# Converting float64 weights on chip: the scaled high words move from SBUF to a PSUM bank

## The chip, the cores and the metric

The kernel runs on one core of one Trainium2 chip. The metric is the device time of one execution in microseconds. One execution was also taken by the hardware profiler, and all rows below come from it. TensorE runs the matmuls and transposes; VectorE, ScalarE and GpSimd work element by element; SyncE (SP) issues nearly all DMAs. In profile rows the engines are PE (PEld for its weight loads), DVE, ACT, POOL and SP. SBUF is the working memory. PSUM has eight banks of 128 partitions by 512 float32; TensorE writes its results there, and VectorE and ScalarE reach it too.

## The reference

A top-k attention feeds two MLPs, one after the other:

```
scores = q k^T / sqrt(64)                    # 4 batches, 8 heads, 576 tokens
keep the 32 largest of each row, softmax over them, times v
x  = attention out as 2304 tokens by 512
x  = relu(x @ w_in)^2 @ w_out                # 512 -> 2048 -> 512
y  = h @ w_out, h = max(0.01 g, g), g = x @ w_in    # second pair of weights
```

q, k and v are float32. The four weight matrices arrive as float64, because the setup scales them by a float64 number, so the kernel has to make float32 of them on chip.

## The kernel before

Every operand of a matmul is split in two: a high part, rounded to TensorE's fp32r format, and the rest. Products are the sum of high by high, high by low and low by high.

**Attention.** 144 tiles of 128 query rows are worked in 72 pairs. A pair has 16 slots. In them VectorE finds the 32 largest of 576 scores of each row by four MAX8 (L800) with three MATCH_REPLACE8 (L802) between them. Around this, at fixed slots, come the scores (L278 on TensorE, evicted at L279), the threshold and exponential (L297, L298, L302), the normalisation (L311), the transposes (`pt_main`, four at L316 into one bank, read at L321 and L322; `pt_left`, L329, read at L338 and L339) and the product with v (`av_split`, L388, read at L393 and L394). In the first three units the older form without a split is used (L324, L342, `av` at L377).

**MLPs.** The tokens are six blocks. A block starts as soon as the attention has filled it, and its matmuls run between the attention's slots: for each of 16 chunks `f` of 128 hidden units, 12 matmuls at L552, then the activation (L562 to L573), then the second product (L590 or L592). A generator `moe` hands this out in small portions; `rate` says how many portions go into a slot.

**Weights.** The first block's 32 chunk steps (16 for each MLP) meet their weights as float64. `w_raw` (L462) loads two tiles of 128x512 double words a step into `wraw`, a ring of four. `w_convert_steps` makes float32 of each: ScalarE scales the low words into an integer (L486) and the high words as a float (L487), VectorE joins them in two bit passes (L490, L491), ScalarE rounds the result to its high part (L495) and GpSimd takes the difference (L498). `w_store` (L506, L507) writes the split chunk to DRAM, and later blocks only load it again (L514, L515). A step converts the chunk of two steps ahead. 64 tiles are converted in all, with 128 bit passes.

**Rings and order.** The two words of a conversion live in tiles of the tag `wc`, a ring of `WCB` slots, which the output tiles `y` (L606) share. Attention results in PSUM come from `bank()`, a ring of three banks under the tag `att`:

```
def bank():
    return psum.tile([P, 512], F, tag="att", name="att", bufs=3)
```

Transposes, value products and the scores of the batches that go straight on (other than batch 0) all take theirs there; the other five banks hold `h` and four `acc` from the first block on. Each engine works its instructions in the order that a planner wrote at build time, from priorities and modelled times; at run time only semaphores hold an instruction. `behind("dve")` puts the first bit pass behind the top-k instruction that was current when the code reached it, and `CONVP` gives conversions a lead in priority.

Of the kernel before, what the change touches and what calls it, by code (L numbers as in the profile page):

```python
# [8 lines left out]
F = mybir.dt.float32  # L9
R = mybir.dt.float32r  # L10
U = mybir.dt.uint32
AF = mybir.ActivationFunctionType
OP = mybir.AluOpType
# [6 lines left out]
H_SCALE = 2.0 ** -112  # L20
# [28 lines left out]
NS = 6  # L49
NE = 4  # L50
WRB = 4
WCB = 5
KRB = 1
VTB = 2

# [15 lines left out]
def topk_attention_moe_moe2_kernel(  # L71
# [12 lines left out]
    P = 128  # L84
# [8 lines left out]
    PE, ACT, DVE, POOL, SP = nc.tensor, nc.scalar, nc.vector, nc.gpsimd, nc.sync  # L93

    const = ctx.enter_context(tc.tile_pool(name="const", bufs=1))
    pool = ctx.enter_context(tc.tile_pool(name="work", bufs=2))
# [3 lines left out]
    def bank():  # L100
        return psum.tile([P, 512], F, tag="att", name="att", bufs=3)
# [7 lines left out]
    def behind(key):  # L109

        return tc.issue_after(cur[key].ins) if key in cur else ExitStack()
# [15 lines left out]
    for u in units:  # L127
        for hp in range(NHP):
# [4 lines left out]
            for t in range(2 * n // P):  # L133
                lo, hi = t * P, t * P + P
# [312 lines left out]
    def w_alloc(i):  # L447
        wi = pool.tile([P, 2, 512], R, tag="wi", name="wi", bufs=3)
        wo = pool.tile([P, 2, 512], R, tag="wo", name="wo", bufs=4)
        wt[i] = (wi, wo)  # L450
        return wi, wo
# [16 lines left out]
    def w_convert(i):  # L468
        g = w_convert_steps(i)
        while True:  # L470
            with tc.high_priority(offset=CONVP):
                if next(g, 1):
                    return
            yield

    def w_convert_steps(i):
        if i >= len(steps) or not fresh[i]:
            return
        w2 = w_alloc(i)
        for raw, w in zip(wraw.pop(i), w2):  # L480
            if W64:
                lo, hi = raw[:, :, 0], raw[:, :, 1]
                c = pool.tile([P, 512], F, tag="wc", name="wc", bufs=WCB)
                cu = c.bitcast(U)
                b = pool.tile([P, 512], U, tag="wc", name="wb", bufs=WCB)
                ACT.activation(b, lo, AF.Copy, scale=L_SCALE, bias=L_BIAS)  # L486
                ACT.activation(c, hi.bitcast(F), AF.Copy, scale=H_SCALE)  # L487
                yield 0
                with behind("dve"):
                    DVE.scalar_tensor_tensor(b, cu, 3, b, op0=OP.logical_shift_left, op1=OP.bitwise_or)  # L490
                DVE.scalar_tensor_tensor(cu, cu, 0x80000000, b, op0=OP.bitwise_and, op1=OP.bitwise_or)  # L491
                yield 0
            else:
                c = raw
            ACT.activation(w[:, 0, :], c, AF.Copy)  # L495
            yield 0
            with behind("pool"):
                POOL.tensor_tensor(w[:, 1, :], c, w.bitcast(F)[:, 0, :], op=OP.subtract)  # L498
            yield 0
# [30 lines left out]
    def moe(j, layer):  # L530
# [69 lines left out]
        for c in range(na):  # L600
# [4 lines left out]
            else:  # L605
                y = pool.tile([P, 512], F, tag="wc", name="y", bufs=WCB)  # L606
                ACT.activation(y, acc[c], AF.Copy)
# [18 lines left out]
    for uh in uhs:  # L626
        b, hp, i = uh["b"], uh["hp"], uh.get("di")
# [248 lines left out]
```

## Time and profile before

| | |
|---|---|
| time, median of 3 runs | 1259.81 us (1259.77 to 1260.94) |
| the profiled execution's own time | 1260.58 us |
| its span | 1258.8 us |
| TensorE busy | 1153.8 us, 92% |
| VectorE busy | 1001.0 us, 80% |
| ScalarE busy | 930.4 us, 74% |
| GpSimd busy | 761.4 us, 60% |
| mean granted TensorE clock | 0.96 |

A line of the kernel in a row (L490) is the line of the code above. `wb<-wc,wb` names the tile that is written and those that are read. Rows by line and shape give the count, the busy time in us and the mean ns of one instruction, then the engine's idle time just before them and what ended it. Rows of a timeline give start and duration in us. In rows of waits stand the total in us, how often, and the longest.

### The profile page before, as it was taken

Reading aid. Unit: us, or ns where it says so; the run is one execution under the profiler, and the core shown is the slowest. Engines: PE = TensorE matmul, PEld = TensorE weight load, DVE = VectorE, ACT = ScalarE, POOL = GpSimd, SP = SyncE. Lnnn points to the kernel's source line nnn. Section 1 sums busy time; section 2 is a strip of 40 time slices with the busy share of each in tenths; the row PEclk is TensorE's granted clock in tenths of the full one; section 3 lists DMA queues with packets and bytes.
Section 4 is the critical chain, followed back from the end, with each engine's and each line's share of the span. In section 5 each row is a group of like instructions: output and inputs, shape, how many; then the busy total and the mean of one; then the engine's idle time right before and its main releaser. Section 6 shows DMA issues by size and latency. Waiting matters only on the chain.

```text
span 1258.8 us, 20236 instructions
## 1 busy us (share of the span) xinstructions
PE 1153.8 (92%) x6352; PEld 1003.9 (80%) x6352; DVE 1001.0 (80%) x1944; ACT 930.4 (74%) x2031; POOL 761.4 (60%) x856
## 2 busy tenths in 40 slices
PE   4888877999868988998999999999999999999998
PEld 3666755787646776997899989888878889999897
DVE  7999999899999999899999999999999810111022
ACT  6999989899888896887788787877777754433322
POOL 7977697488778998447765576654466732003300
PEclk9889885999989998998999999999999999999999
DMA  9745468578776675898998878876666569878974
GB/s 309 259 166 202 155 230 275 191 268 287 254 253 220 234 241 179 286 341 262 374 367 289 298 260 285 281 237 230 214 206 217 190 235 362 285 251 318 358 258 142
DMA packets 110522, 323.24 MB, mean 257 GB/s; under 512 B 17488, under 2 KB 25680, under 8 KB 110416
## 3 DMA queue, kind: packets, MB, share of 16 engines
q1 hardware_dynamic: 107776, 317.24, 73.2%
q10 hardware_dynamic: 2640, 4.72, 1.0%
q8 instruction: 51, 0.84, 0.3%
q14 instruction: 55, 0.45, 0.1%
HBM read 254.54 MB, written 67.37 MB: 256 GB/s over the span
## 4 chain that ended last, share of the span: by engine, by line
PE 53%; DVE 28%; ACT 4%; issue 2%; DMA 2%; POOL 2%; ACTq 0%; POOLq 0%; DVEq 0%
PE h L552 22%; PE acc L592 12%; PE acc L590 9%; DVE m L800 8%; DVE w L802 7%; DVE wb L490 5%; DVE wc L491 4%; PE att L388 3%; PE att L316 3%; PE att L377 2%; DVE PTs L322 2%; PE sp L278 1%; PE att L329 1%; DMA sd<-stage 1%; DMA wo<-wd 1%
## 5 line engine op out<-in xcount | busy, mean ns | idle before, releaser
L552 PE MATMUL h<-xh,wi 128*128 128x512 f32 (+2 forms) x1280 | 349.4, 346 | 5.3 <-ACT ga L562 3.3
L800 DVE MAX8 m<-w 128x8 f32<-128x576 f32 x432 | 314.8, 748 | 1.8
L552 PEld LDWEIGHTS h<-xh,wi 128*128 128x128 f32 x1280 | 228.5, 192 | 33.3 <-ACT ga L562 3.7
L573 POOL TENSOR_TENSOR gl<-ga,gh 128x512 fp32r<-128x512 f32 (+2 forms) x160 | 168.8, 1055 | 125.7 <-ACT gh L572 67.3
L298 POOL TENSOR_TENSOR e<-s,e 128x576 f32<-128x576 f32 x144 | 210.2, 1480 | 39.9 <-ACT e L297 38.5
L802 DVE MATCH_REPLACE8 w<-m,w 128x576 f32<-128x576 f32 x288 | 213.0, 742 | 0.6
L552 PE MATMUL h<-xl,wi 128*128 128x512 f32 (+2 forms) x640 | 207.7, 343 | 2.1 <-DVE xl L604 1.9
L590 PE MATMUL acc<-gh,wo 128*128 128x512 f32 (+2 forms) x768 | 156.2, 344 | 2.3 <-ACT gh L572 2.1
L571 POOL TENSOR_TENSOR ga<-ga,gb 128x512 f32<-128x512 f32 (+2 forms) x80 | 84.4, 1055 | 116.4 <-ACT gb L570 116.0
L592 PE MATMUL acc<-wo,gh 128*128 128x512 f32 x576 | 152.0, 398 | 2.8 <-ACT gh L572 2.6
L590 PEld LDWEIGHTS acc<-gh,wo 128*128 128x128 f32 x768 | 126.6, 190 | 13.5 <-ACT gh L572 3.4
L552 PEld LDWEIGHTS h<-xl,wi 128*128 128x128 f32 x640 | 121.9, 192 | 15.1 <-DVE xl L604 4.2
L572 ACT ACTIVATE gh<-ga 128x512 fp32r<-128x512 f32 (+2 forms) x192 | 100.3, 522 | 35.7 <-POOL ga L571 24.1
L297 ACT ACTIVATE e<-s,kf 128x576 f32<-128x576 f32 x144 | 107.1, 780 | 20.1 <-POOL kf L290 14.4
L592 PEld LDWEIGHTS acc<-wo,gh 128*128 128x128 f32 x576 | 103.7, 188 | 22.6 <-ACT gh L572 4.8
L302 ACT ACTIVATE e<-e,kf 128x576 f32<-128x576 f32 x144 | 112.2, 780 | 11.6 <-POOL e L298 8.3
L311 ACT ACTIVATE e<-e,rc 128x576 f32<-128x576 f32 x144 | 104.4, 776 | 14.9 <-DVE rc L307 14.8
L562 ACT ACTIVATE ga<-h 128x512 f32<-128x512 f32 (+2 forms) x96 | 46.8, 487 | 85.3 <-PE h L552 81.5
L800 DVE MAX8 m<-s 128x8 f32<-128x576 f32 x144 | 105.2, 747 | 5.8 <-ACT s L279 5.6
L802 DVE MATCH_REPLACE8 w<-m,s 128x576 f32<-128x576 f32 x144 | 106.9, 743 | 0.6
L316 PE MATMUL att<-ident,e 128*128 128x128 f32 x576 | 92.0, 291 | 10.3 <-DVE xf L394 5.8
L278 PE MATMUL sp<-KTa,q 128*128 128x288 f32 x320 | 72.0, 355 | 28.7 <-ACT stage L279 22.3
(89 smaller groups left out, 2225.1 us busy)
## 6 DMA issues: line engine op xcount, KB each, us to landing
wi<-wd SPq DMA_DIRECT2D x160, 512.0 KB, 5.2
wo<-wd SPq DMA_DIRECT2D x160, 512.0 KB, 5.4
wraw<-in_w_dram SPq DMA_DIRECT2D x64, 512.0 KB, 4.8
sd<-stage SPq DMA_DIRECT2D x72, 288.0 KB, 3.1
s<-sd SPq DMA_DIRECT2D x72, 288.0 KB, 5.0
wd<-wi SPq DMA_DIRECT2D x32, 512.0 KB, 3.8
wd<-wo SPq DMA_DIRECT2D x32, 512.0 KB, 3.6
kraw<-in_k_dram SPq DMA_DIRECT2D x16, 576.0 KB, 4.6
```

The source lines that it names most:

```text
L297: ACT.activation(e, x, AF.Relu, bias=pr["kf"][:, i:i + 1], scale=-FAR)
L298: cur["pool"] = POOL.tensor_tensor(e, x, e, op=OP.subtract)
L302: ACT.activation(e, e, AF.Exp, bias=pr["nb"][:, i:i + 1], scale=0.125, accum_out=pr["sum"][:, i:i + 1])
L311: ACT.activation(e, e, AF.Copy, scale=pr["rc"][:, i:i + 1])
L316: PE.transpose(ps[:, j * P:(j + 1) * P], t["e"][:, j * P:(j + 1) * P], ident)
L552: PE.matmul(h[:, 0:n], lhsT=wi[:, w, c * P:(c + 1) * P], rhs=x[c][y][:, 0:n], start=cnt == 0, stop=cnt == 3 * NK - 1)
L572: ACT.activation(gh[:, 0:n], a[:, 0:n], AF.Copy)
L573: (DVE if j >= GLD else POOL).tensor_tensor(gl[:, 0:n], a[:, 0:n], gh.bitcast(F)[:, 0:n], op=OP.subtract)
L590: PE.matmul(acc[c][:, 0:n], lhsT=wo[:, w, cs], rhs=g[:, 0:n], start=first, stop=last)
L592: PE.matmul(acc[c], lhsT=g[:, cs], rhs=wo[:, w, :], start=first, stop=last)
L800: cur["dve"] = DVE.max(out=m8[:, x, 8 * r:8 * r + 8], in_=t["s"] if r == 0 else t["w"])
L802: cur["dve"] = DVE.match_replace(out=t["w"], in_to_replace=m8[:, x, 8 * r:8 * r + 8], in_values=t["s"] if r == 0 else t["w"], imm_value=NEG)
```

## The change

The scaled high words no longer go to an SBUF tile but to a bank of the attention's three. The low words keep a tile of the ring `wc`, in which both bit passes now write; each pass reads one PSUM and one SBUF operand where it read two SBUF operands. A conversion takes one slot of `wc` where it took two, and the ring has four slots in place of five. `c`, which L495 and L498 read, is now that SBUF tile seen as float32.

```
-WCB = 5
+WCB = 4
...
-                c = pool.tile([P, 512], F, tag="wc", name="wc", bufs=WCB)
-                cu = c.bitcast(U)
-                b = pool.tile([P, 512], U, tag="wc", name="wb", bufs=WCB)
+                b = pool.tile([P, 512], U, tag="wc", name="wc", bufs=WCB)
+                v = bank()
                 ACT.activation(b, lo, AF.Copy, scale=L_SCALE, bias=L_BIAS)
-                ACT.activation(c, hi.bitcast(F), AF.Copy, scale=H_SCALE)
+                ACT.activation(v, hi.bitcast(F), AF.Copy, scale=H_SCALE)
                 yield 0
+                vu, c = v.bitcast(U), b.bitcast(F)
                 with behind("dve"):
-                    DVE.scalar_tensor_tensor(b, cu, 3, b, op0=OP.logical_shift_left, op1=OP.bitwise_or)
-                DVE.scalar_tensor_tensor(cu, cu, 0x80000000, b, op0=OP.bitwise_and, op1=OP.bitwise_or)
+                    DVE.scalar_tensor_tensor(b, vu, 3, b, op0=OP.logical_shift_left, op1=OP.bitwise_or)
+                DVE.scalar_tensor_tensor(b, vu, 0x80000000, b, op0=OP.bitwise_and, op1=OP.bitwise_or)
                 yield 0
```

## Rows read from the trace of the kernel before

**Rows 1.** By stretch: busy us of PE, PEld, DVE, ACT, POOL; clock, DMA share, GB/s.

```profile
164.00:495.00 331.00, 277.90 (x1304) 220.53 (x1304) 319.48 (x517) 289.94 (x607) 273.84 (x232) 0.92 0.71 243
495.00:1000.00 505.00, 496.94 (x2883) 444.30 (x2882) 490.75 (x1030) 394.07 (x832) 306.72 (x369) 0.99 0.79 273
```

**Rows 2.** Chain that ended last, by line: 164 to 495, then 495 to 1259.

```profile
by line: DVE m L800 19.7%; DVE wb L490 18.3%; DVE w L802 17.8%; DVE wc L491 17.0%; issue 4.8%; DVE PTs L322 3.2%; PE att L377 3.1%; PE h L552 2.0%; DMA sd<-stage 1.8%; DVE PTs L339 1.1%; PE att L278 1.0%; DVE xf L394 0.9%; ACT wi L495 0.9%;
...
by line: PE h L552 35.6%; PE acc L592 19.8%; PE acc L590 14.9%; PE att L388 4.5%; DVE m L800 4.5%; DVE w L802 4.2%; PE att L316 3.4%; issue 1.6%; DVE PTs L322 1.2%; DMA wo<-wd 1.2%; POOL e L298 1.1%; PE att L329 1.0%; DMA wi<-wd 0.9%; PE at
```

**Rows 3.** TensorE's waits from 164 to 495 us.

```profile
PE att L278 <- DVE PTs L322: 13.1, 7, 5.5
```

**Rows 4.** VectorE's groups by line and shape, whole span.

```profile
L490 DVE SCALAR_TENSOR_TENSOR wb<-wc,wb 128x512 uint32<-128x512 uint32 x64 | 72.5, 1133 | 6.4 <-ACT wc L487 6.3
L322 DVE TENSOR_TENSOR PTs<-att,PTs 128x512 fp32r<-128x512 f32 x108 | 72.4, 678 | 3.4 <-ACT PTs L321 2.5
L491 DVE SCALAR_TENSOR_TENSOR wc<-wc,wb 128x512 uint32<-128x512 uint32 x64 | 70.2, 1098 | 0.5
...
L573 DVE TENSOR_TENSOR gl<-ga,gh 128x384 fp32r<-128x384 f32 x32 | 17.9, 559 | 62.6 <-ACT gh L572 60.7 <-issue 1.8
...
L604 DVE TENSOR_TENSOR xl<-acc,xh 128x384 fp32r<-128x384 f32 x4 | 2.1, 547 | 0.0
```

**Rows 5.** Lines L490 and L487: ns min/median/max, first and last start.

```profile
L490 DVE SCALAR_TENSOR_TENSOR wb<-wc,wb x64: 661/1118/1925, 164.2 to 489.4; 128x512 uint32<-128x512 uint32 x64
...
L487 ACT ACTIVATE wc<-wraw x64: 646/673/727, 25.7 to 484.9; 128x512 f32<-128x512 f32 x64
```

**Rows 6.** Timeline, two bit passes and a GpSimd instruction.

```profile
316.94 0.67 DVE L490 SCALAR_TENSOR_TENSOR wb<-wc,wb 128x512 uint32<-128x512 uint32 x1
317.01 1.74 POOL L573 TENSOR_TENSOR gl<-ga,gh 128x512 fp32r<-128x512 f32 x1
...
317.71 1.59 DVE L491 SCALAR_TENSOR_TENSOR wc<-wc,wb 128x512 uint32<-128x512 uint32 x1
```

**Rows 7.** Users of the tag att, 164 to 495 us, counts behind x.

```profile
L316 PE MATMUL att<-ident,e x128: 270/273/476, 176.4 to 486.2; 128*128 128x128 f32 x128
...
L279 ACT ACTIVATE s<-att x56: 388/411/503, 199.7 to 494.4; 128x288 f32<-128x288 f32 x56
...
L329 PE MATMUL att<-ident,e x30: 270/272/423, 177.9 to 470.0; 128*64 128x128 f32 x30
...
L393 ACT ACTIVATE tmp<-att x9: 376/381/438, 280.2 to 481.5; 64x256 f32<-64x256 f32 x8, 64x320 f32<-64x320 f32 x1
```

**Rows 8.** Timeline, first and last users of some banks, and one conversion.

```profile
176.37 1.76 PE L316 MATMUL att<-ident,e 128*128 128x128 f32 x7 [0.48 <-ACT e L311]
...
179.85 0.63 ACT L324 ACTIVATE PT<-att 128x512 f32<-128x512 f32 x1
...
304.86 0.60 PE L316 MATMUL att<-ident,e 128*128 128x128 f32 x4
...
308.89 1.07 ACT L321 ACTIVATE PTs<-att 128x512 fp32r<-128x512 f32 x2
...
311.23 0.71 ACT L487 ACTIVATE wc<-wraw 128x512 f32<-128x512 f32 x1
...
314.33 0.69 DVE L322 TENSOR_TENSOR PTs<-att,PTs 128x512 fp32r<-128x512 f32 x1
...
315.08 0.53 PE L278 MATMUL att<-KT,q 128*128 128x288 f32 x2 [0.24 <-DVE PTs L322]
...
316.34 0.39 ACT L279 ACTIVATE s<-att 128x288 f32<-128x288 f32 x1
...
316.59 1.11 PE L388 MATMUL att<-PTs,VT 128*128 128x256 f32 x8
...
333.18 0.41 DVE L394 TENSOR_TENSOR xf<-att,tmp 64x256 f32<-64x256 f32 x1
```

**Rows 9.** Users of the tag att, 0 to 164 us.

```profile
L324 ACT ACTIVATE PT<-att x26: 592/631/664, 34.6 to 162.5; 128x512 f32<-128x512 f32 x26
```

## Prediction, written before the change was run

> **What bounds the kernel now.** I first read the table of busy times by stretch, to find the stretch in which the change acts. All 128 bit passes lie between 164 and 492 us, so I cut the span at 164 and 495. In these 331 us VectorE is busy for 319.5, ScalarE for 289.9, TensorE for 277.9 (at a granted clock of 0.92) and GpSimd for 273.8; from 495 to 1000 TensorE is busy for 496.9 of 505 us [rows 1]. So VectorE leads up to 495 and TensorE afterwards. The chain of work that ended last, read by stretch, says the same. Up to 495 us its two largest owners besides the top-k lines L800 and L802 are the bit passes, L490 with 18.3% and L491 with 17.0%; behind 495 the MLP matmuls L552, L590 and L592 hold 70% [rows 2]. Together the passes are 35% of the chain in the stretch, some 117 of 331 us, and what is saved there should move everything behind it forward, because TensorE then has a fixed queue of matmuls and no gap to lose the gift in. Last I read the waits in the stretch: the longest of TensorE's are 13.1 us in which score matmuls wait for a bank that VectorE's L322 has not released [rows 3]. So the other engines' gaps, too, are VectorE being late.
>
> **The two passes.** They take 72.5 and 70.2 us, 1133 and 1098 ns each [rows 4], together 142.7 us. The mean hides two speeds: L490's shortest is 661 ns and its longest 1925 [rows 5]. The timeline shows when which comes: the pass at 316.94 us began just ahead of GpSimd's L573 (317.01) and took 0.67; the next, at 317.71, began while that L573 was running (until 318.75) and took 1.59 [rows 6]. It would have ended at 318.4 undisturbed and ended at 319.30, 0.6 behind the GpSimd instruction. So a pass over two SBUF tiles that starts under a running GpSimd instruction is held up until that is through. After the change each pass reads one tile from PSUM and one from SBUF. The nearest row of that kind and size is L322, 128x512 from a bank and an SBUF tile: 108 of them, mean 678 ns, in stretches where GpSimd is busy for 274 of 331 and 307 of 505 us [rows 1, 4]. I take 678 for both passes: 128 x 0.678 = 86.8 us, so VectorE gives back 142.7 - 86.8 = 55.9 us. Bounds: at the shortest pass, 661 ns, it is 58.1; if the stretching stayed as it is, nothing. I take the first end, since 108 rows of the same operands show no slow kind. A loss from the operand itself I exclude, by the next comparison.
>
> Does reading PSUM cost VectorE more? At 128x384, L573 reads two SBUF tiles and takes 559 ns (VectorE runs that line in the last block alone, by the constant GLD, behind the attention); L604 reads a bank and an SBUF tile and takes 547 [rows 4]. So the move costs the operation nothing. [...]
>
> **ScalarE.** L487 writes the bank instead of an SBUF tile. No row shows ScalarE writing PSUM; the nearest is L487 itself, 646 to 727 ns, median 673 [rows 5]. I keep 673; the ends are worth -1.7 and +3.5 us over 64. L495 and L498 read the result in SBUF as before, so they keep their price. The smaller ring (four slots in place of five) now serves one tile a conversion where it served two, four conversions in place of two and a half: no wait comes from it, and part of the waits for L491 at L486 and L487 should go. The DMAs of a step are the same; the loads at L462 reuse a raw tile when L487 has read it, so if L487 waits for a bank, SP's queue waits too, with the stores L506 and L507 and all else behind it.
>
> **GpSimd** gets back what the passes took from it; it is not a bound, so I count nothing.
>
> **What is late next.** Were VectorE alone the bound, the stretch would fall to 331 - 55.9 = 275 us. But ScalarE has 289.9 us of work in it and TensorE 277.9, so the gain is cut at 331 - 290 = 41. VectorE reached 96.5% of the stretch; ScalarE is fed by all the others, and I allow it 95%: 289.9 / 0.95 = 305, a gain of 26 us. Ends: 41 (no idle) and 0.
>
> **The banks.** This is the new cost: a wait for one of three banks, at L487 on ScalarE and in front of every attention matmul on TensorE, in whose queue the MLP's matmuls stand behind. The rows bound it. In the stretch there are 32 groups of four transposes, 15 pairs at L329, 56 score halves and 9 value products [rows 7]; the unsplit products at L377 I leave out. How long does each keep its bank? A transpose group from 176.37 to 180.48 us: 4.1; another from 304.86 until L322 ended at 315.02: 10.2. A score half from 315.08 to 316.73: 1.65. A value product from 316.59 to 333.59: 17 [rows 8]. A conversion would have kept one from L487 at 311.23 [rows 8] until the second pass ended at 319.30 [rows 6]: 8.1, or 7.2 with passes 0.44 us shorter each. Three banks offer 3 x 331 = 993 us. With the long holds, and pairs like transposes, the sum is 47 x 10.2 + 56 x 1.65 + 9 x 17 + 64 x 7.2 = 1186, that is 395 us of stretch: 64 us slower. With the short ones (4.1, 1.65, 4.1 for a value product, and 4.1 for a conversion, an estimate) it is 193 + 92 + 37 + 262 = 584, or 195 us, hidden. The middle is 885, 295 us, just at ScalarE's floor. I take the middle or better, since the long holds are mostly waits for VectorE (L322 ran 5.4 us behind the eviction of the same group), and VectorE is what gets faster; and since a conversion that waits has cover: the code converts two steps ahead of the matmuls, and 64 conversions in 331 us make a step of two 10.3 us, so some 20 us.
>
> **Sum.** The profiled execution took 1260.6 us (span 1258.8), 0.8 over the median of 1259.8. 1260.6 - 26 = 1234.6; I say 1234.
>
> **Rivals.** (a) *Banks decide, slower.* 176 groups share 993 bank-us, 5.6 us each; above that mean hold the stretch grows. At 6.2 us it is 364 us, 33 more than now, and the time 1294. For it: the 10.2 and 17 above, and TensorE's present waits for banks [rows 3]. Against: those holds come out of VectorE's lateness. [...] (b) *Early holds.* The first two conversions' high words are written from 25.7 us on, the first pass comes at 164.2 [rows 5]. If banks are taken as early, two of three are gone for 138 us; the 26 transpose groups of that time [rows 9] at 4.1, 13 pairs as long and some 20 us of products, 180 in all, would have to pass through one, so some 42 lost and 26 won: about 1277. Against: a bank comes from a ring that the attention uses all the time, not from a free buffer. (c) *VectorE's whole gain:* ScalarE's floor does not hold, because part of its 290 us (the score evictions that only fill a store for later) moves behind 495, where it is busy for 394 of 505 us [rows 1]: down to 1260.6 - 55.9 = 1205, so 1205 to 1221. (d) *The banks take most of it:* 1247 to 1262.
>
> **Chances.** Forecast, 1222 to 1246: 0.52. (c) 0.08. (d) 0.17, of which 0.08 is faster by over 0.2% and 0.09 within 0.2% (2.5 us, about what a measurement of this kernel can tell from no change). (a) 0.17 and (b) 0.06, both slower. So faster 0.68, same 0.09, slower 0.23. The range reaches from (c) to the near part of (a): 1211 to 1270, which leaves out about 0.06 below and 0.13 above. The forecast's own range is 1222 to 1246.
>
> **What would show it.** Right: both passes near 678 ns with no slow kind; the conversion ends near 469 instead of 495; VectorE's share in it falls below 90% while ScalarE's rises to about 95%; behind it TensorE stays full and the two kernels run parallel. Wrong: passes above 900 ns would break the first term; ScalarE idle at L487, released by L491 or L322, or TensorE idle in front of L278, L316 and L388 for more than some 50 us, means that the banks decide; L487 of the first conversions far ahead of their passes means (b).

## The result, and the profile after

The changed kernel takes 1221.9 us (median of 4 runs, 1220.9 to 1225.3) against 1259.8 for the kernel before: a ratio of 0.971 (95% interval 0.968 to 0.973), 38 us faster. The forecast was 1234, its own range 1222 to 1246, the whole range 1211 to 1270; the median lies at the lower edge of the forecast's own range. The profiled execution took 1220.9 us, its span is 1219.1.

VectorE's groups by line and shape come first, in the columns of [rows 4]:

```profile
L322 DVE TENSOR_TENSOR PTs<-att,PTs 128x512 fp32r<-128x512 f32 x108 | 72.7, 678 | 5.4 <-ACT PTs L321 4.6
L490 DVE SCALAR_TENSOR_TENSOR wc<-att,wc 128x512 uint32<-128x512 uint32 x64 | 43.4, 682 | 23.4 <-ACT att L486 22.7 <-POOL ga L571 0.3
L491 DVE SCALAR_TENSOR_TENSOR wc<-att,wc 128x512 uint32<-128x512 uint32 x64 | 43.2, 680 | 0.5
```

The passes fell from 1133 and 1098 ns to 682 and 680, 142.7 us to 86.6. The slow kind is gone altogether, as the rows by line show (ns min/median/max; L486 is now the line that writes the high words, L487 before):

```profile
L490 DVE SCALAR_TENSOR_TENSOR wc<-att,wc x64: 657/681/692, 184.8 to 437.3; 128x512 uint32<-128x512 uint32 x64
...
L491 DVE SCALAR_TENSOR_TENSOR wc<-att,wc x64: 660/679/692, 186.9 to 438.0; 128x512 uint32<-128x512 uint32 x64
...
L486 ACT ACTIVATE att<-wraw x64: 603/646/704, 183.2 to 436.6; 128x512 f32<-128x512 f32 x64
```

The last pass starts at 438.0 us. In the kernel before, the same line ran

```profile
L491 DVE SCALAR_TENSOR_TENSOR wc<-wc,wb x64: 666/1067/1912, 168.5 to 491.8; 128x512 uint32<-128x512 uint32 x64
```

so the conversions are done 54 us sooner. The first two high words no longer run 138 us ahead of their passes: L486 starts at 183.2, L490 at 184.8.

Busy time by stretch, in the columns of [rows 1]; 456 lies as far from the end as 495 did before:

```profile
164.00:456.00 292.00, 267.01 (x1298) 217.05 (x1296) 240.67 (x461) 274.14 (x577) 224.81 (x226) 0.96 0.83 285
456.00:961.00 505.00, 492.70 (x2870) 439.92 (x2871) 498.92 (x1052) 397.40 (x846) 306.89 (x365) 0.99 0.79 267
```

From these points on TensorE has the same work left. The rest of each span is, before and then after,

```profile
1000.00:1259.00 259.00, 252.72 (x1528) 236.65 (x1527) 36.34 (x68) 100.30 (x225) 49.84 (x62) 1.00 0.77 272
```

```profile
961.00:1219.00 258.00, 252.31 (x1535) 237.19 (x1534) 50.38 (x99) 105.77 (x236) 52.16 (x65) 1.00 0.77 271
```

that is 2883 + 1528 = 4411 matmuls before [rows 1] and 2870 + 1535 = 4405 after.

VectorE is down from 97% to 82% of the first stretch, and ScalarE, from 88 to 94%, is the busiest. In the second, TensorE and VectorE are both over 97%. VectorE's largest waits up to the end of the attention are now (total us, times, longest):

```profile
DVE wc L490 <- ACT att L486: 22.7, 14, 3.3
DVE m L800 <- ACT s L279: 22.2, 14, 5.0
```

Both are VectorE waiting for ScalarE. In the kernel before, the first was 6.3 us [rows 4], and the second was

```profile
DVE m L800 <- ACT s L279: 5.6, 7, 1.8
```

The 13.1 us of score matmuls waiting for a bank behind L322 [rows 3] came down to this, in the same view:

```profile
PE att L278 <- DVE PTs L322: 0.7, 1, 0.7
```

And the banks come back sooner. Over the stretch, from the first matmul into a bank to the end of its last reader, the mean hold is 7.8 us before (20 groups) and 4.0 after (16) for the transposes that L321 and L322 read, 13.6 (9) and 4.0 (7) for value products, and 3.1 for a conversion. In the timeline of the kernel after, a transpose group holds one from 342.06 to 346.42, 4.4 us (10.2 in [rows 8]), and a value product from 331.45 to 334.96, 3.5 us (17 before):

```profile
331.45 1.34 PE L388 MATMUL att<-PTs,VT 128*128 128x256 f32 x9 [0.18 <-DVE PTs L339]
...
334.56 0.40 DVE L394 TENSOR_TENSOR xf<-att,tmp 64x256 f32<-64x256 f32 x1
...
342.06 0.63 PE L316 MATMUL att<-ident,e 128*128 128x128 f32 x4 [2.17 <-DVE wc L491]
...
345.76 0.66 DVE L322 TENSOR_TENSOR PTs<-att,PTs 128x512 fp32r<-128x512 f32 x1
```

The bracket in the third line shows that lending has a price, though: these transposes waited 2.17 us for a bank that a second pass had just let go. In the whole stretch such waits of TensorE's come to 2.9 us.

**Where the 38 us come from.** A cut at the end of the attention (VectorE's last MAX8) parts them. The busy times from 0 to that point, before and then after, in the columns of [rows 1]:

```profile
0.00:1000.00 1000.00, 901.06 (x4825) 767.27 (x4826) 964.63 (x1877) 830.12 (x1807) 711.60 (x795) 0.95 0.74 253
```

```profile
0.00:976.00 976.00, 901.93 (x4893) 771.92 (x4894) 910.51 (x1878) 830.14 (x1817) 678.31 (x801) 0.97 0.77 262
```

The attention ends 24 us sooner: VectorE has 54 us less to do, and 30 us more idle (1000 - 964.6 = 35 before, 976 - 910.5 = 65 after). In those 24 us less, TensorE has done 68 matmuls more, at a higher granted clock (0.97 for 0.95). So what is left for it after the attention is shorter too: 243 us of span in place of 259. 24 + 16 = 40, the difference of the spans. The cut at 495 and 456 us above puts it otherwise: there TensorE has the same work left, and the whole difference, 331 - 292 = 39 us, lies ahead of the cut. What moved is the attention against TensorE's other work: the first MAX8 of 27 tiles starts in the stretch in place of 31, and the MLP's matmuls run there instead.

### The profile page after: what moved, and what is told of

The parts are those of the page before. It is cut to its first block, busy times and chain, and to the rows that moved or that the text cites. A ratio compares the mean times of both kernels' runs of the same rounds, so it can differ in the third digit from the quotient of the medians.

```text
span 1219.1 us, 20275 instructions
## 1 busy us (share of the span) xinstructions
PE 1139.2 (93%) x6352; PEld 996.5 (82%) x6352; DVE 946.1 (78%) x1944; ACT 924.7 (76%) x2031; POOL 721.0 (59%) x856
## 5 line engine op out<-in xcount | busy, mean ns | idle before, releaser
L573 POOL TENSOR_TENSOR gl<-ga,gh 128x512 fp32r<-128x512 f32 (+2 forms) x160 | 162.9, 1018 | 124.5 <-ACT gh L572 44.5
L298 POOL TENSOR_TENSOR e<-s,e 128x576 f32<-128x576 f32 x144 | 203.3, 1432 | 42.1 <-ACT e L297 39.7
L571 POOL TENSOR_TENSOR ga<-ga,gb 128x512 f32<-128x512 f32 (+2 forms) x80 | 81.4, 1018 | 114.2 <-ACT gb L570 113.9
L316 PE MATMUL att<-ident,e 128*128 128x128 f32 x576 | 88.6, 285 | 10.0 <-ACT e L311 4.5
L278 PE MATMUL sp<-KTa,q 128*128 128x288 f32 x320 | 68.8, 350 | 25.6 <-ACT stage L279 21.2
```

What stands on the lines that cost most here:

```text
L298: cur["pool"] = POOL.tensor_tensor(e, x, e, op=OP.subtract)
L316: PE.transpose(ps[:, j * P:(j + 1) * P], t["e"][:, j * P:(j + 1) * P], ident)
L573: (DVE if j >= GLD else POOL).tensor_tensor(gl[:, 0:n], a[:, 0:n], gh.bitcast(F)[:, 0:n], op=OP.subtract)
```

## Experiments

Each is a short edit of the kernel before or after, run beside the kernel before on the same chip; the ratio is to that kernel, whose median was 1259.2 to 1260.6 us. Two theories were to be told apart. *Relief*: a pass over two SBUF tiles is held up by GpSimd, one with a PSUM operand is not, and VectorE bounds the stretch of conversions. *Ring*: the gain comes from a conversion taking one slot of `wc` instead of two. A third, *order*, was that the planner's new order made it; every edit brings a new order, so no run tests it by itself.

**Half of the change, pass 1.** The low words go to a bank, the high words stay in SBUF; two slots of `wc` a conversion, as before:

```
+                v = bank().bitcast(U)
-                ACT.activation(b, lo, ...)
+                ACT.activation(v, lo, ...)
-                    DVE.scalar_tensor_tensor(b, cu, 3, b, ...)
+                    DVE.scalar_tensor_tensor(b, cu, 3, v, ...)
```

> Half of the change, from the kernel before: the low words go to a bank and the high words stay in SBUF, so pass 1 reads one PSUM and one SBUF tile, pass 2 still two SBUF tiles; the ring wc serves two tiles a conversion as before. Theory (the passes are held up by GpSimd only when both operands lie in SBUF, and VectorE bounds the stretch): pass 1 near 680 ns, pass 2 near 1100, VectorE gets back 64 x 0.45 = 29 us, the time falls to 1230 to 1242. Rival ring (the gain of the change is that a conversion needs one slot of wc where it needed two): nothing, 1256 to 1262. Rival order (the planner's new order made the gain): no forecast, but the durations would not have to follow the operands.

1232.1 us, ratio 0.978 (0.976 to 0.979).

```profile
L492 DVE SCALAR_TENSOR_TENSOR wc<-wc,wb 128x512 uint32<-128x512 uint32 x64 | 70.5, 1101 | 0.7
L491 DVE SCALAR_TENSOR_TENSOR wb<-wc,att 128x512 uint32<-128x512 uint32 x64 | 43.4, 677 | 14.3 <-ACT att L487 13.3 <-POOL VT L232 0.7
```

**The other half, pass 2.** Both words stay in SBUF; pass 1 writes a bank, and pass 2 reads it:

```
+                v = bank().bitcast(U)
-                    DVE.scalar_tensor_tensor(b, cu, 3, b, ...)
+                    DVE.scalar_tensor_tensor(v, cu, 3, b, ...)
-                DVE.scalar_tensor_tensor(cu, cu, 0x80000000, b, ...)
+                DVE.scalar_tensor_tensor(cu, cu, 0x80000000, v, ...)
```

> The other half, from the kernel before: both words stay in SBUF, pass 1 reads two SBUF tiles and writes a bank, pass 2 reads that bank and one SBUF tile. Theory: pass 1 stays near 1100 ns, pass 2 falls to about 680, VectorE gets back 64 x 0.42 = 27 us, the time falls to 1232 to 1244, and the two halves together are a little more than the whole change gave, since the whole is cut by ScalarE. Rival ring: 1256 to 1262.

1232.7 us, ratio 0.979 (0.977 to 0.981).

```profile
L491 DVE SCALAR_TENSOR_TENSOR att<-wc,wb 128x512 uint32<-128x512 uint32 x64 | 65.3, 1023 | 5.9 <-ACT s L279 3.1 <-ACT wc L487 2.2
L492 DVE SCALAR_TENSOR_TENSOR wc<-wc,att 128x512 uint32<-128x512 uint32 x64 | 43.0, 674 | 0.9
```

In both runs the duration follows the operands: the pass that reads one PSUM tile takes 674 to 677 ns, the pass over two SBUF tiles stays above 1000. Each half wins 28 us with the ring as it was, so the ring is not needed for the gain and relief stands: VectorE's passes took 29 and 34 us less. Two different orders that each win 28 us speak against *order* as the main cause, but do not exclude it as a part. Together they win 56, the whole change 38: the second half is worth less once the first is there.

**GpSimd kept from reading.** The kernel before, with GpSimd writing zeros where it subtracted for the low parts of the weights (L498) and of the hidden values (L573, in all blocks but the last, where VectorE has it); these low parts are left out of the result:

```
-                POOL.tensor_tensor(w[:, 1, :], c, w.bitcast(F)[:, 0, :], op=OP.subtract)
+                POOL.memset(w.bitcast(F)[:, 1, :], 0.0)
...
+                    POOL.memset(gl.bitcast(F)[:, 0:n], 0.0)
```

> The kernel before, both words in SBUF, but GpSimd writes zeros where it took the low parts of the weights (L498) and of the hidden values (L573): it leaves those two low parts out, so only the durations of the passes are read. GpSimd's instructions that read SBUF then fill some 135 of the 331 us in place of 274. Theory (a pass over two SBUF tiles is held up by a GpSimd instruction that is reading SBUF): the part above 670 ns about halves, mean 850 to 950 ns. Rival (two SBUF operands are slow beside any traffic, whoever makes it): mean stays 1050 to 1130.

The means are 835 and 867 ns, one below the range that was given and one in it. The medians show that it is not every pass that became a little faster:

```profile
L490 DVE SCALAR_TENSOR_TENSOR wb<-wc,wb x64: 665/679/1918, 164.2 to 449.6; 128x512 uint32<-128x512 uint32 x64
...
L491 DVE SCALAR_TENSOR_TENSOR wc<-wc,wb x64: 664/683/1928, 168.6 to 451.0; 128x512 uint32<-128x512 uint32 x64
```

More than half of the passes now take the short time over two SBUF tiles, with 1.92 us still the longest. So two SBUF operands are not slow by themselves; what GpSimd does beside them decides. The starts and ends in the traces say it pass by pass. In the kernel before, 89 of the 128 passes take over 0.70 us; each began while a GpSimd instruction that reads SBUF was running, and ended 0.54 to 0.56 us behind it. The 24 that began with GpSimd free took at most 0.69; of the other 15 short ones, 11 began in the last 0.15 us of a GpSimd instruction and 4 in its first 0.2. In this run 24 passes began under a zero fill (0.30 to 0.56 us), and the longest took 0.69: none of them was held up. All 31 that took over 0.70 began under an instruction that reads. In the changed kernel 100 of the 128 began under one, and the longest took 0.69. The one run of this kernel took 1227.3 us; as work is left out, that time is no price of the passes.

**VectorE loaded further.** A third pass, pass 2 done again, in each kernel (here the kernel before; in the kernel after the line with `b` and `vu` is doubled):

```
                 DVE.scalar_tensor_tensor(cu, cu, 0x80000000, b, ...)
+                DVE.scalar_tensor_tensor(cu, cu, 0x80000000, b, ...)
```

> The kernel before with pass 2 done twice (the second time changes no bit). The third pass reads two SBUF tiles too, so 64 x 1.1 = 70 us more for VectorE. If VectorE bounds the kernel before in the stretch of conversions, as the forecast has it, the time grows by most of that: 1305 to 1335. If it were one bound among several there: 1275 to 1295. The same edit to the kernel after cost 20 us for 44 us of VectorE.

In the kernel before: 1322.4 us, ratio 1.050 (1.047 to 1.053), 63 us slower.

```profile
L490 DVE SCALAR_TENSOR_TENSOR wb<-wc,wb 128x512 uint32<-128x512 uint32 x64 | 67.9, 1062 | 0.7 <-ACT wc L487 0.7
L491 DVE SCALAR_TENSOR_TENSOR wc<-wc,wb 128x512 uint32<-128x512 uint32 x64 | 63.5, 993 | 0.2
L492 DVE SCALAR_TENSOR_TENSOR wc<-wc,wb 128x512 uint32<-128x512 uint32 x64 | 62.9, 982 | 0.1
```

The three take 194.3 us, 51.6 more than two did, and cost 63: more than one for one. VectorE bounds the kernel before there, as the forecast had it, with almost no wait left in front of the passes; why it is more than one for one stays open. The cut at the attention's end shows the rest:

```profile
0.00:1033.00 1033.00, 899.93 (x4716) 764.20 (x4717) 1007.02 (x1940) 825.39 (x1793) 707.76 (x786) 0.93 0.71 240
1033.00:1320.00 287.00, 279.26 (x1638) 257.73 (x1636) 36.53 (x69) 108.57 (x239) 61.47 (x71) 0.99 0.76 263
```

The attention ends 33 us later, and 109 matmuls more stand behind it, 287 us of span for 259. It is the picture of the change with the sign turned.

> The kernel after with pass 2 done twice (the second time changes no bit): 64 x 0.68 = 44 us more for VectorE in the stretch of conversions, and each bank kept 0.7 us longer. Theory (VectorE is no longer the bound, ScalarE is): VectorE had about 50 us of room there, so the time grows by 0 to 15 us, 1222 to 1237. Rival (VectorE still bounds the stretch): it grows by some 35 to 45 us, 1257 to 1267.

In the kernel after: 1242.0 us, ratio 0.985 (0.984 to 0.987), 20 us slower than the change for 43.3 us of VectorE. Neither figure that was given: VectorE is neither free there nor the only bound. The profiled execution of this run took 1249.1 us, 7 above its median. In it VectorE's idle time up to the attention's end stayed what it was (61 us for 65, in the table further below): the waits for ScalarE were not slack that a further pass could fill.

**The ring, shorter.** The kernel after with `WCB = 3` and `WCB = 2`:

> The kernel after with three slots of wc in place of four: three conversions in flight, the nearest to the two and a half of before. With two, 20 of the 38 us were lost, because ScalarE waits for a free slot before the low words. If the gain rests on the ring as well as on the passes: 1228 to 1236. If two was only below a threshold and the passes gave all: 1220 to 1226.

> The kernel after with two slots of wc in place of four: two conversions in flight, fewer than the two and a half of before (the output tiles y share the two slots). Theory: the ring is not what gave the gain, 1220 to 1230. Rival ring: most of the gain is lost, 1245 or more.

Three slots: 1229.7 us, ratio 0.977 (0.974 to 0.979). Two: 1241.8, ratio 0.986 (0.984 to 0.989). VectorE's waits from 164 to 455 us with two slots:

```profile
DVE wc L490 <- ACT wc L485: 30.8, 17, 3.7
```

L485 writes the low words into the ring, and with two slots it comes too late. Three in flight are the nearest to the two and a half of before, and 8 of the 38 us are gone with them. So the ring has a part: by these runs some 30 us come without it, and some 8 with the fourth conversion in flight. No run had exactly two and a half.

**The ring, longer.** Five slots, and the roundings of head pairs 8 to 15 on GpSimd as in a run further below:

```
-WCB = 4
+WCB = 5
-HI_SET = (0, 1, ..., 15)
+HI_SET = (0, 1, ..., 7)
```

> The kernel after with five slots of wc, as many as before had, and the roundings of head pairs 8 to 15 on GpSimd as in the run that came to 1220. If a longer ring lets ScalarE run further ahead of VectorE: 1208 to 1217. If four slots were already enough: 1218 to 1223.

1236.0 us, ratio 0.981 (0.979 to 0.984): a miss, and 16 us worse than the same with four slots (1220.1). ScalarE's waits from 164 to 455 us, with five slots and then with four:

```profile
ACT wc L485 <- DMA wraw<-in_w_dram: 28.4, 22, 2.5
```

```profile
ACT wc L485 <- DMA wraw<-in_w_dram: 4.2, 6, 1.4
```

With five slots ScalarE reaches L485 22 times before its raw tile has landed, with everything else of ScalarE behind it. The loads themselves take no longer (median 5.3 us from issue to landing, 5.8 in the changed kernel, with four slots); the ring `wraw` still has four tiles. That the order with a fifth slot puts the low words too early fits this, but is not shown.

**The banks.** Conversions on a bank of their own and two for the attention (kernel after), and two for the attention with conversions in SBUF (kernel before):

```
-        return psum.tile([P, 512], F, tag="att", name="att", bufs=3)
+        return psum.tile([P, 512], F, tag="att", name="att", bufs=2)
...
-                v = bank()
+                v = psum.tile([P, 512], F, tag="hw", name="hw", bufs=1)
```

> The kernel after with the three banks parted: one for conversions alone, two for the attention. Theory (banks are hidden now that VectorE is on time): 1216 to 1235. Rival (the three banks are close to the bound, and sharing all three is what keeps it hidden): 1240 or more, with TensorE waiting in front of the attention's matmuls.

> The kernel before with two banks for the attention in place of three, conversions in SBUF as before: the price of a bank to the attention alone. If banks are loose: within 5 us of 1260. If they are tight, as the long holds of before say: 1270 to 1300.

Own bank: 1260.0 us, ratio 1.000 (0.999 to 1.002), the whole gain gone. Two banks in the kernel before: 1280.8, ratio 1.016 (1.014 to 1.018). A bank is thus worth 20 us to the attention without any conversion. The last rows of MAX8 show the end of the attention, for own bank and for two banks:

```profile
L800 DVE MAX8 m<-w x432: 731/749/764, 11.4 to 1029.9; 128x8 f32<-128x576 f32 x144
```

```profile
L800 DVE MAX8 m<-w x432: 729/750/769, 11.2 to 1047.3; 128x8 f32<-128x576 f32 x144
```

With its own bank the passes are as short as in the change, and the last conversion is done by 457 us, 18 later; the last MAX8 starts at 1030 us in place of 975, 55 later. So the loss lies mostly behind the conversions, where the bank set aside stands idle. Of VectorE's waits from 455 to 1031 us the largest is one that the change does not have,

```profile
DVE m L800 <- DMA s<-sd: 24.3, 16, 5.5
```

The run with two banks has it too (14.4 us); why these loads come late with two banks stays open. So the gain needs the three to be shared: the conversions borrow from them for some 255 us, and the attention has all three for the rest.

**ScalarE relieved.** In the kernel after, the score evictions of batch 1 on VectorE, and, apart from that, the roundings of q, k and v of head pairs 8 to 15 on GpSimd (the `HI_SET` edit above, with four slots):

```
+        if direct(uh) and uh["b"] == 1:
+            DVE.tensor_copy(t["s"][:, ks], ps[:, 0:HALF])
+        else:
             ACT.activation(t["s"][:, ks], ps[:, 0:HALF], AF.Copy)
```

> The kernel after with the score evictions of batch 1 (L279, 72 of 0.41 us, about 47 of them in the stretch of conversions) on VectorE in place of ScalarE: 20 us less for ScalarE, about as much more for VectorE, in the stretch. Theory (ScalarE bounds the stretch at 94 to 99% busy): 1205 to 1216. Rival (the gain of the change ended at TensorE or at banks): 1219 to 1226. If VectorE were still the bound: 1235 or more.

> The kernel after with the roundings of q, k and v for head pairs 8 to 15 (L115) on GpSimd in place of ScalarE: about 10 us less for ScalarE in the stretch, about as much more for GpSimd. Theory (ScalarE bounds the stretch, GpSimd has 67 of 292 us free): 1212 to 1220. Rival (ScalarE is not the bound): 1220 to 1228.

Evictions on VectorE: 1229.0 us, ratio 0.976 (0.973 to 0.979), 7 us slower than the change. Roundings on GpSimd: 1220.1 us, ratio 0.968 (0.965 to 0.971), not to be told from the change. The first misses what was forecast for ScalarE as the bound; the second lies where that forecast and its rival meet, at 1220. It is a weak test, though: the edit took 9 us from ScalarE in all and only some 5 of them (274.1 to 268.6) in the stretch, where 10 were expected. With the roundings moved, VectorE's waits from 164 to 455 us were

```profile
DVE wc L490 <- ACT att L486: 22.9, 19, 4.1
DVE m L800 <- ACT s L279: 8.3, 11, 1.7
```

The wait for scores fell by 13 us (21.0 in the same view after), the wait for high words stayed. None of the versions beats the change by more than the measurement's spread.

The cut at the end of the attention, from the busy times of each profiled execution (us):

| kernel | attention ends | VectorE busy until then | idle | span behind it |
|---|---|---|---|---|
| before | 1000 | 965 | 35 | 259 |
| pass 1 alone | 985 | 935 | 50 | 245 |
| after | 976 | 911 | 65 | 243 |
| after, roundings on GpSimd | 973 | 912 | 61 | 243 |
| after, evictions on VectorE | 989 | 935 | 54 | 239 |
| after, third pass | 1008 | 947 | 61 | 239 |
| after, own bank | 1031 | 917 | 114 | 229 |
| before, third pass | 1033 | 1007 | 26 | 287 |

## Why the prediction was right, and where its size was off

The direction and the mechanism held, step by step.

*VectorE bounds the stretch.* Shown: 52 us more of it cost 63, and each half of the relief won 28.

*The two passes.* 678 ns was forecast, 682 and 680 came; 55.9 us given back was forecast, 56.1 came. That GpSimd's reading is the cause is shown by the starts and ends of the passes, and by the run in which it reads less. GpSimd got its part back as well, 761 us busy before and 721 after, and L498 took 1456 ns (mean) before and 1295 after; no run shows what that alone is worth. A PSUM operand costs the operation nothing: 681 and 679 ns, where the 24 passes of the kernel before that began with GpSimd free took at most 691 over two SBUF tiles, and the medians in the run with zero fills are 679 and 683.

*ScalarE's write.* L486 is 28 ns shorter than the line it replaces (647 for 675 ns mean, 1.8 us in all), just past the lower end of what was allowed (1.7).

*The ring.* The forecast said that no wait comes from it, and counted nothing. By the run with three slots it was worth some 8 us: a term put at nothing.

*The banks.* "The middle or better" was the right choice: nearly the forecast's short holds came, a mean of 4.0 us for transposes, 4.0 for a product and 3.1 for a conversion, where it had 4.1 for each. The reason given, waits for VectorE, holds for the larger part. Of the 3.9 us that the transposes' hold lost, 2.6 lie between the end of ScalarE's eviction and the end of L322, the rest ahead of the eviction. That banks are scarce all the same is shown by the two runs with one fewer. Rivals (a) and (b) fell: no stretch grew, and the first conversions take their banks 1.6 us ahead of the first pass.

*The other engines' gaps.* "So the other engines' gaps, too, are VectorE being late" was read from one row. Of the 53 us that TensorE waited in the stretch before, VectorE ended 29 and ScalarE 21, the largest of these

```profile
PE sp L278 <- ACT stage L279: 10.1, 8, 2.5
```

so ScalarE was late there already.

*ScalarE as the next bound, and the sum.* Here the size was off, 26 us forecast and 38 measured. The step that was mis-sized is the floor of 289.9 us, with which the forecast made 289.9 / 0.95 = 305 us of the stretch. It came to 292, with 274.1 us of ScalarE's work at 94%: attention work of about four tiles was done later, so part of rival (c) came true. "What is saved there should move everything behind it forward" held for TensorE, which has 4411 and 4405 matmuls left 763 us before the end. It did not hold for the attention, which moved by 24 us only; the conversions, forecast to end near 469 us, were done at 439. VectorE saved 54 us up to the attention's end, and 30 came back as idle time, mainly the two waits for ScalarE (44.9 us against 11.9). That these 24 us lie near the 26 of the forecast is chance: the forecast spoke of the stretch. The third pass in the kernel before moves the same two amounts the other way, 33 us up to the attention's end and 28 behind it.

Whether ScalarE's load is the floor stays open. It is the busiest engine of the stretch, and VectorE's new waits are for it, but 5 us less of it there gave nothing that can be told. Open is also why ScalarE delivers the high words late, 23 us of VectorE's waits in either case. Its place in the planner's order and its load would both do it, and no run parts them.

## What to carry to other kernels

When one engine's instruction shows two durations for one shape, look for what runs beside it before costing the instruction: here the slow kind vanished by moving one of two operands to PSUM, at the same 680 ns for every pass. When the engine that is late also holds a scarce buffer, take the hold times from after its relief, not from before. And an engine's work in a stretch is a floor only if none of it can be done later: here four tiles of attention moved out of the stretch, and it came to 292 us where 305 was forecast.

## What the runs showed of the hardware that was not expected

The 128 passes with one PSUM operand lie between 657 and 692 ns while GpSimd is busy for 77% of the stretch, with not one exception. A copy of 128x288 from PSUM takes VectorE 448 ns (median), longer than ScalarE's 411 [rows 7], though over the 72 that were moved this is only 3 of the 7 us that moving them cost. And a longer ring can be slower: five slots against four cost 16 us, with ScalarE's waits for its loads up from 4 to 28 us.
